# A T5 attention and snake-MLP kernel on one core: regrouped first loads, band rows from a DRAM table, float32 values cast on POOL, two tokens a row, full-row warm-up

## Chip, cores and metric

The kernel runs on one core of one Trainium2 chip. The metric is the device time of one execution in microseconds (us). Engines: PE is TensorE, PEld its weight loads, DVE VectorE, ACT ScalarE, POOL GpSimd, SP the engine that here only issues loads and stores (SPq, ACTq, POOLq: the queue side of an engine). "Granted clock" is the share of TensorE's full clock that the throttle allowed.

## The reference

```python
# attention: q, k, v are [8 batches, 8 heads, 576 tokens, 64], float32
scores = (q @ k.T) / sqrt(64) + bias_table[bucket(|i - j|)]     # 32 buckets
attn   = softmax(scores);  o = attn @ v                         # per batch and head
# MLP over the 4608 tokens x 512: w_in [512, 2048], w_out [2048, 512]
h   = x @ w_in
g   = h + sin(alpha * h) ** 2 / alpha
out = g @ w_out                                                 # float32
```

## The kernel before

It takes the batches one after the other, each as four pairs of heads. It multiplies the exponentials of the raw scores by exponentials of the bias (DVE), which depend only on i - j: `m2` holds for each head 128 rows of 384 values, row p being a table of 512 values shifted by p ("band rows"); `mh` holds two pieces of it rearranged. Batches 0 and 1 have their k and q transposed on PE from natural-order tiles (`nat0`: the first pair, `nat1`: the other pairs of batch 0, `nat2`: batch 1). The order on each engine is set ahead by a planner in the program, which uses estimated durations and a few start times (`T_...`). The parts that the change and the argument touch:

```python
SI = 4; SN = (128, 16); SO = (0, 512)     # 4 tokens to a partition row: 512 + 64 tokens

# --- SP queue: bias table, then k and q of the first pair ---
nc.sync.dma_start(out=tabN, in_=bias_table)
nc.sync.dma_start(out=tabL, in_=...)                        # its last row, 32 times
for kq, src in ((0, k), (1, q)):
    load_nat([x[:, kq] for x in nat0], src[0], 0, 2, eng=nc.sync)
# --- POOL queue (casts float32 to float16 on the way) ---
... nat1, pair 1 ...
load_v16(0)                                                 # values of batch 0
... nat1, heads 4 to 7 ...

def warm(n):                                                # warm-up matmuls, 64 rows
    x = new_mo()
    for _ in range(n):
        nc.tensor.matmul(out=x, lhsT=kzs[0][0:64, 0, S : S + 128],
                         rhs=kzs[0][0:64, 0, S : S + 512], start=True, stop=True)

nc.scalar.activation(out=tabE, in_=tabN, func=AF.Exp)
warm(WARM0)
nc.tensor.matmul(out=eps_[0:H, 0:EW], lhsT=tabE, rhs=phi_sb, start=True, stop=True)
warm(WARM1)
nc.scalar.activation(out=e_sb, in_=eps_[0:H, 0:EW], func=AF.Copy)   # 8 x 512 table, SBUF
for h in range(H):                                          # 8 loads, SBUF to SBUF
    nc.sync.dma_start(out=m2[:, h, :],
        in_=bass.AP(tensor=e_sb.tensor, offset=e_sb[h : h + 1, 127:128].offset,
                    ap=[[e_sb.ap[0][0], 1], [-1, 128], [1, XW]]))
nc.sync.dma_start(out=alphaN, in_=...)
nc.sync.dma_start(out=idf_sb, in_=idf.ap())
# --- POOL, in order ---
nc.gpsimd.tensor_copy(out=mh[0:64, :, :], in_=me[0:64, 0, :, 0:192])
nc.gpsimd.tensor_copy(out=mh[64:128, :, :], in_=me[64:128, 1, :, 64:256])
load_w_in16()
... nat2 (batch 1), values of batch 1, w_out ...

# --- copies of a transposed k or q tile out of PSUM: one for each row size (128, 16) ---
for j in range(2):
    n, o = SN[j], SO[j]
    pin = c.v[:, o : o + SI * n].rearrange("d (i p) -> d i p", i=SI)
    ...
        copy_on(e, cols(kzs[t], o)[0:64], pin[0:64])
# ... cut: scores, exponentials, averages, MLP, planner
```

The softmax here doesn't subtract the row's maximum and nothing guards it: scores larger than these inputs give would overflow.

## Time and profile before

| quantity (before) | value |
|---|---|
| device time, median of 3 | 489.86 us (488.75 to 490.55) |
| PE busy over the span | 94% |
| PE busy in the first 40 us | 19.3 us |
| a steady batch, 142.26 to 192.89 us | 50.63 us, PE busy 50.48 |
| `mh` copies done | 36.7 us |
| first MoE matmul (`sc<-xT,w_in`) | 68.70 us |

First, three lines of the page's slices. The span is cut in 40 slices of 12.2 us; a digit is the busy share in tenths, for PEclk the granted clock.

```profile
PE   5268979999999999999999999999999999999996
...
PEclk9997979999999999999999999999999999999999
DMA  9969999940990099309960699039001000000021
```

From the seventh slice to the last but one PE is at nine tenths, so a microsecond won in front is won at the end, as long as the later part doesn't change. PE had little to do early (5, 2, 6) while the DMA engines looked busy.

The windows view gives PE's busy time, the granted clock, the DMA share and the rate in stretches: the first 40 us, the MoE-in stage of batch 0, and a steady batch.

```profile
core 0: us, PE busy (x) PEld busy (x) DVE busy (x) ACT busy (x) POOL busy (x), PEclk, DMA share, GB/s
0.00:40.00 40.00, 19.34 (x151) 9.59 (x151) 14.86 (x30) 15.34 (x32) 14.04 (x24) 0.95 1.09 81
67.50:89.90 22.40, 21.16 (x138) 9.67 (x139) 19.31 (x34) 18.79 (x32) 7.64 (x7) 0.87 1.99 164
142.26:192.89 50.63, 50.48 (x346) 25.61 (x345) 30.06 (x64) 44.36 (x98) 9.24 (x8) 1.00 0.80 90
```

The chain of waits, cut at 45 us and in order of time (start, length, what): line 405 is the loop of eight band-row loads, line 410 a small load issued behind them.

```profile
4.99 0.60 ACT e_sb L403
...
5.60 0.65 SPq L405
...
8.78 5.97 SPq L405
...
27.28 3.77 SPq L410
...
31.10 4.72 DMA idf_sb<-identf
...
35.87 0.84 POOL mh L414
```

Issuing eight loads kept SP from 5.6 to 27.3 us: five of the eight issues lasted 1.8 to 6.0 us. The profile doesn't name what they waited for; earlier loads are likely, since the eight issues of e12 below took 4.4 us in all. The waits view up to 45 us (engine and line, what was waited for, total us, times, longest) shows who stood still for it:

```profile
POOL mh L413 <- DMA m_77<-e_sb: 23.8, 1, 23.8
...
PE mo L470 <- DMA nat_128_95<-in_k_dram: 8.9, 1, 8.9
...
DVE u L564 <- POOL mh L414: 7.4, 1, 7.4
PE mo L470 <- DVE kz_66 L450: 6.2, 1, 6.2
```

Three microseconds in which little but band rows moves (the DMA view from 24 to 27 us; packets, MB, share of 16 engines):

```profile
DMA packets 155, 0.10 MB, mean 34 GB/s; under 512 B 7, under 2 KB 155, under 8 KB 155
...
q1 hardware_dynamic: 110, 0.08, 73.2%
```

The q1 packets are the band rows: 0.732 x 16 engines x 3 us / 110 = 0.32 us for a packet of 768 bytes in this quiet stretch. Over all 1,024 row packets of the trace the mean is 0.24 us.

### The profile page before, as it was taken

The numbers are of one execution on the slowest core, as the hardware profiler recorded it, in microseconds if no ns is written. First come the engines' busy times: TensorE is split into PE (matmuls) and PEld (weight loads), VectorE is DVE, ScalarE is ACT, GpSimd is POOL, SyncE is SP. The second block draws the span as 40 slices with busy tenths as digits, with TensorE's granted clock in tenths as the row PEclk, the third lists the DMA queues.
The fourth block names the chain that finished last, engine by engine and source line by source line (L and its number), as shares of the span: only waits on it lengthen the run. The fifth ranks groups of instructions, "written<-read, shape, count | busy, mean of one in ns | idle before, by whom it ended". The sixth has DMA issues, their size and how long they took to land.

```text
span 488.1 us, 8297 instructions
## 1 busy us (share of the span) xinstructions
PE 456.9 (94%) x3133; PEld 229.1 (47%) x3133; DVE 277.5 (57%) x580; ACT 388.7 (80%) x838; POOL 83.3 (17%) x88
## 2 busy tenths in 40 slices
PE   5268979999999999999999999999999999999996
PEld 2134434455445544554455545554455445544442
DVE  4229568645674468445854494449544864479700
ACT  4255979987898879887997799779987998799711
POOL 7016774000700061004300340012000000000000
PEclk9997979999999999999999999999999999999999
DMA  9969999940990099309960699039001000000021
GB/s 119 96 27 174 152 184 153 178 85 23 176 159 24 22 145 158 54 24 105 170 64 21 108 156 92 24 94 145 23 23 44 1 23 21 33 13 0 23 80 71
DMA packets 140295, 40.09 MB, mean 82 GB/s; under 512 B 124336, under 2 KB 135136, under 8 KB 140256
## 3 DMA queue, kind: packets, MB, share of 16 engines
q0 software_dynamic: 100000, 18.06, 48.1%
q1 hardware_dynamic: 40064, 21.45, 22.5%
q8 instruction: 24, 0.39, 0.3%
q14 instruction: 15, 0.12, 0.1%
q10 hardware_dynamic: 192, 0.07, 0.1%
HBM read 36.78 MB, written 16.52 MB: 109 GB/s over the span
## 4 chain that ended last, share of the span: by engine, by line
PE 62%; ACT 24%; issue 6%; SPq 5%; DVE 1%; DMA 1%; POOL 0%; ACTq 0%; DVEq 0%
PE mo L717 20%; PE av L613 15%; PE sc L541 13%; PE sc L669 8%; PE av L607 5%; SPq L405 4%; ACT u L548 4%; ACT L738 3%; ACT sq L683 2%; DMA idf_sb<-identf 1%; PE mo L470 1%; ACT kz_67 L448 1%; SPq L410 1%; DVE kz_67 L450 1%; ACT rd L633 1%
## 5 line engine op out<-in xcount | busy, mean ns | idle before, releaser
L548 ACT ACTIVATE u<-sc 128x384 f16<-128x384 f32 x448 | 173.0, 544 | 17.9 <-PE sc L541 17.7
L717 PE MATMUL mo<-w_out_80,g 128*128 128x512 f16 x576 | 173.7, 379 | 0.0
L669 PE MATMUL sc<-xT,w_in_79 128*128 128x512 f16 x576 | 132.8, 384 | 0.9 <-DVE g L690 0.9
L581 DVE TENSOR_TENSOR u<-u,m_77 128x512 f16<-128x512 f16 (+1 forms) x192 | 71.3, 390 | 72.4 <-ACT u L548 71.2
L690 DVE SCALAR_TENSOR_TENSOR g<-sq,inv_a,sc 128x512 f16<-128x512 f16 x144 | 104.5, 747 | 3.9 <-ACT sq L683 1.1
L669 PEld LDWEIGHTS <-w_in_79 128*128 128x128 f16 x576 | 56.1, 99 | 69.3 <-issue 4.4
L717 PEld LDWEIGHTS <-g 128*128 128x128 f16 x576 | 55.7, 97 | 53.4 <-issue 4.3
L541 PE MATMUL sc<-qT_69,kz_66 128*128 128x384 f16 (+1 forms) x288 | 63.2, 298 | 1.0 <-ACT u L548 0.2
L541 PE MATMUL sc<-qT_70,kz_67 128*128 128x384 f16 (+1 forms) x288 | 63.7, 285 | 0.2
L629 ACT ACTIVATE lnd<-av 128x384 f32<-128x384 f32 x64 | 27.2, 425 | 42.0 <-PE av L613 42.0
L644 DVE TENSOR_TENSOR xT<-av,rd 128x384 f16<-128x384 f32 (+1 forms) x68 | 29.4, 437 | 48.6 <-ACT rd L633 32.6
L613 PE MATMUL av<-u,ones 128*64 128x192 f16 (+1 forms) x512 | 43.8, 293 | 0.0
L334 POOL DMA_DIRECT2D v_72<-in_v_dram x16 | 14.1, 889 | 131.1 <-PE av L613 124.8
L541 PEld LDWEIGHTS <-kz_66 128*128 128x128 f16 x288 | 26.5, 100 | 20.9 <-issue 5.0
L541 PEld LDWEIGHTS <-kz_67 128*128 128x128 f16 x288 | 26.7, 97 | 19.8 <-issue 0.8
L334 POOL DMA_DIRECT2D v_71<-in_v_dram x16 | 15.3, 1106 | 82.9 <-PE av L613 82.8
L450 DVE COPY outs<-mo 128x512 f32<-128x512 f32 x28 | 19.2, 687 | 17.7 <-PE mo L717 17.6
L633 ACT ACTIVATE rd<-lnd 128x384 f32<-128x384 f32 x64 | 28.2, 440 | 1.3
L613 PEld LDWEIGHTS <-ones 128*64 128x64 f16 x512 | 21.7, 109 | 13.4 <-issue 7.4
L613 PE MATMUL av<-u,v_71 128*64 128x384 f16 (+1 forms) x256 | 21.8, 292 | 0.0
L613 PE MATMUL av<-u,v_72 128*64 128x384 f16 (+1 forms) x256 | 21.8, 292 | 0.0
L448 ACT ACTIVATE outs<-mo 128x512 f32<-128x512 f32 x8 | 4.8, 597 | 20.6 <-PE mo L717 20.6
(359 smaller groups left out, 403.8 us busy)
## 6 DMA issues: line engine op xcount, KB each, us to landing
out_dram<-outs SPq DMA_DIRECT2D x36, 256.0 KB, 2.0
staged_k<-in_k_dram POOLq DMA_DIRECT2D x6, 576.0 KB, 13.6
staged_q<-in_q_dram POOLq DMA_DIRECT2D x6, 576.0 KB, 15.8
v_71<-in_v_dram POOLq DMA_DIRECT2D x16, 128.0 KB, 8.1
w_in_79<-in_moe_w_in_dram POOLq DMA_DIRECT2D x4, 512.0 KB, 8.1
v_72<-in_v_dram POOLq DMA_DIRECT2D x16, 128.0 KB, 5.4
w_out_80<-in_moe_w_out_dram POOLq DMA_DIRECT2D x4, 512.0 KB, 9.6
kz_66<-kraw SPq DMA_DIRECT2D x3, 288.0 KB, 6.0
```

The source lines that it names most:

```text
L334: nc.gpsimd.dma_start(out=vs[t % 2][:, c], in_=vp[128 * c : 128 * c + 128],)
L541: nc.tensor.matmul(out=sc.v[:, n * y : n * y + n], lhsT=kzs[t % 2][:, p, k0 : k0 + 128], rhs=qTs[t % 2][:, p, q0 : q0 + n], start=True, st ...
L548: nc.scalar.activation(out=u.v[:, k0 : k0 + nc_, q0 : q0 + n], in_=sc.v[:, 0 : n * nc_], func=AF.Exp, scale=0.125,)
L581: nc.vector.tensor_tensor(out=io, in0=io, in1=m2[:, 2 * p : 2 * p + 2, x0 : x0 + hi - lo], op=ALU.mult,)
L607: nc.tensor.matmul(out=o[:, 0:n], lhsT=vhs[t % 2][:, p] if y else ones2, rhs=u.v[:, 8, q0 : q0 + n], start=True, stop=False,)
L613: nc.tensor.matmul(out=o[64 * z : 64 * z + 64, 0:n], lhsT=vs[t % 2][:, c, 2 * p + z, :] if y else ones, rhs=u.v[:, 4 * z + c, q0 : q0 + n] ...
L629: nc.scalar.activation(out=ln.v[:, 0:n], in_=avs[0].v[:, 0:n], func=AF.Ln)
L633: nc.scalar.activation(out=rd.v[:, 0:n], in_=ln.v[:, 0:n], func=AF.Exp, scale=-1.0)
L644: nc.vector.tensor_tensor(out=xT[:, p, (x0 + a) % XN : (x0 + a) % XN + m - a], in0=avs[1].v[:, a:m], in1=rd.v[:, a:m], op=ALU.mult,)
L669: nc.tensor.matmul(out=h.v, lhsT=w_in16[:, j, 128 * f : 128 * f + 128], rhs=xT[:, j, 512 * b % XN : 512 * b % XN + 512], start=(j == 0), s ...
L690: nc.vector.scalar_tensor_tensor(out=gcell[b].v[:, f, :], in0=sq.v, scalar=inv_a[:, f : f + 1], in1=h.v, op0=ALU.mult, op1=ALU.add,)
L717: nc.tensor.matmul(out=m.v, lhsT=gcell[b].v[:, f, 128 * a : 128 * a + 128], rhs=w_out16[:, f, :], start=(f == 0), stop=(f == NF - 1),)
```

## The change

Its intent is to start PE's real work earlier. The small bias table is written to DRAM and the band rows are read from there in one load, in ascending order; POOL then copies them reversed. The first k load goes ahead of the table on SP, q on ACT's queue, `nat1` alone on POOL's queue; the values come as float32 over SP and POOL casts them. k and q rows hold two tokens instead of four, which makes the copies out of PSUM single. Warm-up matmuls use 128 rows. The planner's start times are moved. The diff is cut to its core; several lines are pressed into one in places, and `<...>` or `...` stands for what is left out.

```diff
-T_START = 9.0   T_M2 = 14.0  T_V0 = 15.0  T_TR1 = 38.0  T_W = 33.0  T_WO = 56.0
+T_START = 8.0   T_M2 = 13.0  T_V0 = 17.0  T_TR1 = 36.0  T_W = 28.0  T_WO = 50.0
-    SI = 4;  SN = (128, 16);  SO = (0, 512)
+    SI = 2;  SN = (128, 128, 32);  SO = (0, 256, 512)
+    e_dram = nc.dram_tensor("e_dram", [H, EW], F16, kind="Internal")
+    # vst, vhst (float32 values) and m2r (rows): room in w_out16, which is loaded later
+    def cast_v(eng, t):
+        for c in range(4):
+            eng.tensor_copy(out=vs[t][:, c], in_=vst[:, c])
+        ...
+    def warm(n):                    # zz: 128 x 512 zeros
+            nc.tensor.matmul(out=x, lhsT=zz[:, 0:128], rhs=zz, start=True, stop=True)
+    load_nat(nat0, 0, 0, 2, k[0], nc.sync)          # ahead of tabN, tabL
     nc.sync.dma_start(out=tabN, in_=bias_table)
     nc.sync.dma_start(out=tabL, ...)
+    load_nat(nat0, 1, 0, 2, q[0], nc.scalar)
     ... nat1 on POOL ...
-    load_v16(0)
-    nc.scalar.activation(out=e_sb, in_=eps_[0:H, 0:EW], func=AF.Copy)
-    for h in range(H):
-        nc.sync.dma_start(out=m2[:, h, :], in_=<e_sb, partition h, rows descending>)
+    nc.vector.tensor_copy(out=e_sb, in_=eps_[0:H, 0:EW])
+    nc.sync.dma_start(out=e_dram.ap(), in_=e_sb)
+    nc.sync.dma_start(
+        out=m2r, in_=bass.AP(tensor=e_dram, offset=0, ap=[[1, 128], [EW, H], [1, XW]]))
+    load_v32(0, nc.sync)
+    for p in range(NP):
+        nc.gpsimd.tensor_copy(
+            out=m2[:, 2 * p : 2 * p + 2, :], in_=m2r[:, 2 * p : 2 * p + 2, ::-1])
     nc.gpsimd.tensor_copy(out=mh[0:64, ...)  ; nc.gpsimd.tensor_copy(out=mh[64:128, ...)
+    cast_v(nc.gpsimd, 0)
     load_w_in16()
     ... nat2 ...
     # copies out of PSUM: one over all 576 tokens
-        for j in range(2): ... copy_on(e, cols(kzs[t], o)[0:64], pin[0:64]) ...
+        put(kzs[t][:, p, 0:S], slice(0, 64), 0, 288)
     # ... cut: casts of the first pair, memsets moved to POOL, values of batch 1
```

More of the change, by code (lines that the diff above doesn't have):

```diff
@@ L160 @@
 OFFSET = 8
-T_START = 9.0
-T_M2 = 14.0
-T_V0 = 15.0
-T_TR1 = 38.0
-T_W = 33.0
-T_WO = 56.0
+T_START = 8.0
+T_M2 = 13.0
+T_V0 = 17.0
+T_TR1 = 36.0
+T_W = 28.0
+T_WO = 50.0
 WARM0 = 5
@@ L210 @@
     WIN = ((0, 384), (384, 192))
-    SI = 4
-    SN = (128, 16)
-    SO = (0, 512)
+    SI = 2
+    SN = (128, 128, 32)
+    SO = (0, 256, 512)
     XN = 1536
@@ L246 @@
     w_out16 = sgl.tile([128, NF, DM], F16, name="w_out16")
+    wv = w_out16.rearrange("p f n -> p (f n)")
+    vst = wv[:, 0 : 2 * 4 * H * D].bitcast(F32).rearrange("p (c h d) -> p c h d", c=4, h=H)
+    vhst = wv[:, 2 * 4 * H * D : 2 * 4 * H * D + 2 * NP * D].bitcast(F32).rearrange(
+        "p (hp d) -> p hp d", hp=NP
+    )
+    m2r = wv[:, 2 * 5 * H * D : 2 * 5 * H * D + H * XW].rearrange("p (h x) -> p h x", h=H)
+    zz = sgl.tile([128, 512], F16, name="zz")
     alphaT = sgl.tile([128, NF], F32, name="alphaT")
@@ L264 @@
     natx = tp.tile([128, NF * DM], F16, name="natx", tag="g", bufs=2)
-    N0 = 2 * 2 * SI * D
-    nat0 = [
-        natx[0:n, 2 * N0 * i : 2 * N0 * (i + 1)].bitcast(F32).rearrange(
-            "s (kq h x) -> s kq h x", kq=2, h=2
-        )
-        for i, n in enumerate(SN)
-    ]
-    natb = [
-        natx[0:n, 4 * N0 + N0 * i : 4 * N0 + N0 * (i + 1)].rearrange(
-            "s (kq i two d) -> s kq i two d", kq=2, i=SI, two=2
-        )
-        for i, n in enumerate(SN)
-    ]
-    nat2x = tp.tile([128, NF * DM], F16, name="nat2", tag="g", bufs=2)
-    N2 = 2 * H * SI * D
-    nat2 = [
-        nat2x[0:n, N2 * i : N2 * (i + 1)].rearrange("s (kq h x) -> s kq h x", kq=2, h=H)
-        for i, n in enumerate(SN)
-    ]
-    nat1 = [sgl.tile([n, 2, H - 2, SI * D], F16, name=f"nat1_{n}") for n in SN]
+    N0 = 3 * 2 * 2 * SI * D
+    nat0 = natx[:, 0 : 2 * N0].bitcast(F32).rearrange(
+        "s (j kq h x) -> s j kq h x", j=3, kq=2, h=2
+    )
+    natb = natx[:, 2 * N0 : 3 * N0].rearrange(
+        "s (j kq i two d) -> s j kq i two d", j=3, kq=2, i=SI, two=2
+    )
+    nat2x = tp.tile([128, NF * DM], F16, name="nat2", tag="g", bufs=2)
+    nat2 = nat2x[:, 0 : 3 * 2 * H * SI * D].rearrange(
+        "s (j kq h x) -> s j kq h x", j=3, kq=2, h=H
+    )
+    nat1 = sgl.tile([128, 3, 2, H - 2, SI * D], F16, name="nat1")
     def new_g():
@@ L341, in load_v16, with load_v32, load_nat @@
             )
-    def load_nat(dst, src, h0, h1, parts=(0, 1), eng=None):
-        for i in parts:
-            n, o = SN[i], SO[i]
-            (eng or nc.gpsimd).dma_start(
-                out=dst[i],
+    def load_v32(t, eng):
+        vp = v[t].rearrange("h s d -> s h d")
+        for c in range(4):
+            eng.dma_start(out=vst[:, c], in_=vp[128 * c : 128 * c + 128])
+        vq = v[t].rearrange("(hp two) s d -> two s hp d", two=2)
+        for z in range(2):
+            eng.dma_start(out=vhst[64 * z : 64 * z + 64], in_=vq[z, 512:S])
+    def cast_v(eng, t):
+        for c in range(4):
+            eng.tensor_copy(out=vs[t][:, c], in_=vst[:, c])
+        for z in range(2):
+            eng.tensor_copy(
+                out=vhs[t][64 * z : 64 * z + 64, :, z, :], in_=vhst[64 * z : 64 * z + 64]
+            )
+    def load_nat(dst, kq, h0, h1, src, eng, parts=(0, 1, 2)):
+        for j in parts:
+            n, o = SN[j], SO[j]
+            eng.dma_start(
+                out=dst[0:n, j, kq],
                 in_=src[h0:h1, o : o + SI * n].rearrange("h (p i) d -> p h (i d)", i=SI),
@@ L361, in load_w_out16, with clear_v, cast0 @@
             )
-    nc.scalar.dma_start(out=phi_sb, in_=phi_h.ap())
-    nc.scalar.dma_start(out=id_sb, in_=idm.ap())
-    nc.scalar.preload_act_table_set(EXP_SET)
+    def clear_v(eng, i):
+        eng.memset(vhs[i][0:64, :, 1, :], 0.0)
+        eng.memset(vhs[i][64:128, :, 0, :], 0.0)
+    def warm(n):
+        x = new_mo()
+        for _ in range(n):
+            nc.tensor.matmul(out=x, lhsT=zz[:, 0:128], rhs=zz, start=True, stop=True)
+    def cast0(kq, j, eng):
+        n = SN[2 * j]
+        for jj in (0, 1) if j == 0 else (2,):
+            o = natb[0:n, jj, kq]
+            i_ = nat0[0:n, jj, kq].rearrange("s two (i d) -> s i two d", i=SI)
+            if eng is nc.scalar:
+                eng.activation(out=o, in_=i_, func=AF.Copy)
+            else:
+                eng.tensor_copy(out=o, in_=i_)
+    load_nat(nat0, 0, 0, 2, k[0], nc.sync)
     nc.sync.dma_start(out=tabN, in_=bias_table)
@@ L371 @@
     )
+    nc.scalar.dma_start(out=phi_sb, in_=phi_h.ap())
+    load_nat(nat0, 1, 0, 2, q[0], nc.scalar)
+    nc.scalar.dma_start(out=id_sb, in_=idm.ap())
+    nc.scalar.preload_act_table_set(EXP_SET)
     for kq, src in ((0, k), (1, q)):
-        load_nat([x[:, kq] for x in nat0], src[0], 0, 2, eng=nc.sync)
+        load_nat(nat1[:, :, :, 0:2], kq, 2, 4, src[0], nc.gpsimd, parts=(0, 1))
     for kq, src in ((0, k), (1, q)):
-        load_nat([x[:, kq, 0:2] for x in nat1], src[0], 2, 4, parts=(0,))
+        load_nat(nat1, kq, 2, H, src[0], nc.gpsimd, parts=(2,))
     for kq, src in ((0, k), (1, q)):
-        load_nat([x[:, kq] for x in nat1], src[0], 2, H, parts=(1,))
-    load_v16(0)
-    for kq, src in ((0, k), (1, q)):
-        load_nat([x[:, kq, 2:6] for x in nat1], src[0], 4, H, parts=(0,))
+        load_nat(nat1[:, :, :, 2:6], kq, 4, H, src[0], nc.gpsimd, parts=(0, 1))
+    nc.vector.memset(zz, 0.0)
     nc.vector.memset(kzs[0][0:64, :, S : 2 * S], 0.0)
-    def warm(n):
-        x = new_mo()
-        for _ in range(n):
-            nc.tensor.matmul(
-                out=x, lhsT=kzs[0][0:64, 0, S : S + 128], rhs=kzs[0][0:64, 0, S : S + 512],
-                start=True, stop=True,
-            )
-    def clear_v(eng, i):
-        eng.memset(vhs[i][0:64, :, 1, :], 0.0)
-        eng.memset(vhs[i][64:128, :, 0, :], 0.0)
-    nc.vector.memset(kzs[0][64:128, :, 0:S], 0.0)
     nc.vector.tensor_tensor(out=tabN, in0=tabN, in1=tabL, op=ALU.subtract)
@@ L402 @@
     warm(WARM1)
-    nc.scalar.activation(out=e_sb, in_=eps_[0:H, 0:EW], func=AF.Copy)
-    for h in range(H):
-        nc.sync.dma_start(
-            out=m2[:, h, :],
-            in_=bass.AP(tensor=e_sb.tensor, offset=e_sb[h : h + 1, 127:128].offset,
-                        ap=[[e_sb.ap[0][0], 1], [-1, 128], [1, XW]]),
-        )
+    nc.vector.tensor_copy(out=e_sb, in_=eps_[0:H, 0:EW])
+    nc.sync.dma_start(out=e_dram.ap(), in_=e_sb)
+    cast0(0, 0, nc.vector)
+    cast0(1, 0, nc.scalar)
+    cast0(0, 1, nc.vector)
+    cast0(1, 1, nc.scalar)
+    nc.vector.memset(kzs[0][64:128, :, 0:S], 0.0)
+    nc.sync.dma_start(
+        out=m2r, in_=bass.AP(tensor=e_dram, offset=0, ap=[[1, 128], [EW, H], [1, XW]])
+    )
+    load_v32(0, nc.sync)
     nc.sync.dma_start(out=alphaN, in_=moe_alpha.rearrange("(f p) -> f p", p=128))
     nc.sync.dma_start(out=idf_sb, in_=idf.ap())
+    clear_v(nc.gpsimd, 0)
+    nc.gpsimd.memset(ones, 1.0)
+    nc.gpsimd.memset(ones2, 0.0)
+    nc.gpsimd.memset(ones2[0:64, 0, :], 1.0)
+    nc.gpsimd.memset(ones2[64:128, 1, :], 1.0)
+    for p in range(NP):
+        nc.gpsimd.tensor_copy(
+            out=m2[:, 2 * p : 2 * p + 2, :], in_=m2r[:, 2 * p : 2 * p + 2, ::-1]
+        )
     me = m2.rearrange("p (hp two) x -> p two hp x", two=2)
@@ L414 @@
     nc.gpsimd.tensor_copy(out=mh[64:128, :, :], in_=me[64:128, 1, :, 64:256])
+    cast_v(nc.gpsimd, 0)
     load_w_in16()
     for kq, src in ((0, k), (1, q)):
-        load_nat([x[:, kq] for x in nat2], src[1], 0, H)
+        load_nat(nat2, kq, 0, H, src[1], nc.gpsimd)
+    load_v32(1, nc.sync)
     clear_v(nc.gpsimd, 1)
-    load_v16(1)
     nc.gpsimd.memset(kzs[1][0:64, :, S : 2 * S], 0.0)
     nc.gpsimd.memset(kzs[1][64:128, :, 0:S], 0.0)
+    cast_v(nc.gpsimd, 1)
     load_w_out16()
-    def cast0(kq):
-        for i in range(2):
-            i_ = nat0[i][:, kq].rearrange("s two (i d) -> s i two d", i=SI)
-            if kq == 0:
-                nc.vector.tensor_copy(out=natb[i][:, kq], in_=i_)
-            else:
-                nc.scalar.activation(out=natb[i][:, kq], in_=i_, func=AF.Copy)
-    cast0(0)
-    cast0(1)
-    clear_v(nc.vector, 0)
-    nc.vector.memset(ones, 1.0)
-    nc.vector.memset(ones2, 0.0)
-    nc.vector.memset(ones2[0:64, 0, :], 1.0)
-    nc.vector.memset(ones2[64:128, 1, :], 1.0)
     plan = Plan()
@@ L457, in mm @@
             c.v = new_mo().bitcast(F16)
-            for j in range(2):
-                n, o = SN[j], SO[j]
+            for j in range(3):
+                n = SN[j]
                 for i in range(SI):
-                    x = o + n * i
+                    x = i * (S // 2) + SO[j] // 2
                     if t == 0 and p == 0:
                         nc.tensor.transpose(
-                            out=c.v[:, x : x + n], in_=natb[j][:, kq, i],
+                            out=c.v[:, x : x + n], in_=natb[0:n, j, kq, i],
                             identity=id_sb[0:n, 0:n],
@@ L471, in mm @@
                             out=c.v[64 * z : 64 * z + 64, x : x + n],
-                            in_=(nat1 if t == 0 else nat2)[j][:, kq, h, D * i : D * i + D],
+                            in_=(nat1 if t == 0 else nat2)[0:n, j, kq, h, D * i : D * i + D],
                             identity=id_sb[0:n, 0:n],
@@ L477, in go, with put @@
             def go(e):
-                for j in range(2):
-                    n, o = SN[j], SO[j]
-                    pin = c.v[:, o : o + SI * n].rearrange("d (i p) -> d i p", i=SI)
-                    def cols(tile, c0):
-                        return tile[:, p, c0 : c0 + SI * n].rearrange("d (p i) -> d i p", i=SI)
-                    if kq == 1:
-                        copy_on(e, cols(qTs[t], o), pin)
-                    elif part == 0:
-                        copy_on(e, cols(kzs[t], o)[0:64], pin[0:64])
-                    else:
-                        copy_on(e, cols(kzs[t], (S + 64, S)[j])[64:128], pin[64:128])
+                pin = c.v[:, 0:S].rearrange("d (i p) -> d i p", i=SI)
+                def put(dst, r, p0, p1):
+                    copy_on(
+                        e, dst.rearrange("d (p i) -> d i p", i=SI)[r], pin[r][:, :, p0:p1]
+                    )
+                if kq == 1:
+                    put(qTs[t][:, p, :], slice(0, 128), 0, 288)
+                elif part == 0:
+                    put(kzs[t][:, p, 0:S], slice(0, 64), 0, 288)
+                else:
+                    put(kzs[t][:, p, S + 64 : 2 * S], slice(64, 128), 0, 256)
+                    put(kzs[t][:, p, S : S + 64], slice(64, 128), 256, 288)
             return go
         m = plan.add({"PE": 0.4 if t == 0 and p == 0 else 0.7}, mm, deps, pri, nb, new=[b])
-        eng = {"DVE": 0.95, "ACT": 0.85}
+        eng = {"DVE": 0.75, "ACT": 0.7}
         return [plan.add(eng, cp(x), [m], pri, use=[b]) for x in range(1 if kq else 2)]
```

## The prediction

> **What bounds it now.** By the page's slices TensorE (PE) is saturated from about 40 us to the end (94% of the span; a steady batch takes 50.6 us). The change leaves that part alone. The loss is in front: the windows view gives PE 19.3 us of work in the first 40 us, 5 of it warm-up.
>
> 47% of the chain of waits in the first 45 us is the SP queue issuing eight band-row loads (`m2` from `e_sb`, 5.6 to 27.3 us; each 8.6–15.7 us to landing). POOL stands 23.8 us before the `mh` copies (34.7 us); the band multiply with `mh` waits 7.4 us for them, and pair 2's transposes 6.2 us for in-order DVE: PE resumes at 38.5 us. Earlier PE waits 8.9 us (to 24.8) for `nat1` heads 4–7, queued behind the values. `w_in` and later POOL loads start only at 36.65 us. While only band rows remain (24–27 us), a packet costs 0.32 us (73% of 16 engines x 3 us, 110 packets).
>
> **What changes.**
> - Band rows come from DRAM in one load. 1,024-byte DRAM rows took about 52 ns a packet at 3–6 us; 1,024 packets then take 3–4 us, not 20. Price: a DRAM write (2 us), four reversing POOL copies (0.8 us each, sized like the `mh` copies), a table behind the `k` load. Expected: e_sb at 7.5 us, rows landed 14.5, `mh` 20.
> - Values arrive as float32 on SP and are cast on POOL (3 us), ready near 23 us. `nat1` lands by 13: its wait vanishes.
> - Two tokens a row: 12 transposes instead of 16 per tile (0.15 us less), single copies (0.8 instead of 1.4 us), but twice the packets at half the size. [...] `nat` rows are now written as 256 B, values too. Before, 128-byte rows moved at about 1,000 packets/us at 55–58 us, so no disaster.
> - Full-row warm-up: no time of its own.
>
> **The sum.** First scores at 11.4 instead of 13.6 us. First values product at 23 instead of 30.5; PE then skips the 6.2 us stop and has 2 us of transposes behind it: 15–16 us ahead. The rest of batch 0 stays bound by ACT and PE (first MoE matmul 68.8 us before); 1–2 us come off for slow-clock matmuls and copies. Batch 1's `nat2` follows the value cast and `w_in` on POOL and lands at 42–46 us, when PE wants it at 42–43: I charge 2–3 us. Net 16.4 us; the first MoE matmul comes at about 52 us.
>
> All of it is on the critical path, since PE is saturated afterwards: 489.9 - 16.4 = **473.5 us, 80% range 466 to 482**. Faster by over 2%: 0.86; within 2%: 0.135; slower: 0.005.
>
> **Signs.** Right: band rows leave the chain's head; PE idle before 40 us falls by 10 us or more; no PE wait for `nat1`; `mh` at 18–22 us; `w_in` issued at 22–26; first MoE matmul at 49–56; steady batches unchanged. The granted clock fell to 0.50 after the 6 us stop (36–40 us) and at 68–72; the first dip should go [...]. Wrong: `mh` after 26 us, or first MoE matmul after 60.
>
> **What would make it wrong.** 256-byte float32 packets slow on SP, values after 28 us; reversing or casting copies slower on POOL; `nat2` later than that, PE stopped before the last averages; a lasting clock dip. If none bites, 466.

The sum came to 16.4 us. The 2 us of the DRAM write and the 3 us of the casts are estimates; in the trace before, the stores of 256 KB took 2.0 us from issue to landing and an `mh` copy (64x768) 0.82 us.

## The result, and the profile after

The changed kernel took **472.89 us** (median of 4 runs, 471.44 to 473.53), beside 489.73 us of the kernel before (median of 4). The ratio is 0.9653 with a 95% interval of 0.9623 to 0.9683. Ratios here are the mean time of one kernel's fast runs over that of the other's of the same rounds, so they are not quite the ratio of the medians quoted.

The same slices (now of 11.8 us), windows, chain and waits:

```profile
PE   5688899999999999999999999999999999999996
...
PEclk9989899999999999999999999999999999999999
DMA  9699999409900996049901990094101000100021
```

```profile
core 0: us, PE busy (x) PEld busy (x) DVE busy (x) ACT busy (x) POOL busy (x), PEclk, DMA share, GB/s
0.00:40.00 40.00, 28.54 (x235) 13.83 (x237) 19.87 (x43) 25.02 (x63) 29.27 (x46) 0.96 0.98 176
54.89:73.16 18.27, 17.82 (x119) 8.25 (x120) 15.77 (x29) 17.26 (x28) 8.73 (x8) 1.00 2.06 163
125.73:176.36 50.63, 50.48 (x346) 25.57 (x345) 30.06 (x64) 44.37 (x98) 9.24 (x8) 1.00 0.82 92
44.00:48.00 4.00, 2.27 (x27) 1.27 (x26) 2.32 (x7) 3.70 (x10) 4.00 (x5) 1.00 1.31 164
48.00:52.00 4.00, 3.95 (x26) 1.54 (x26) 0.00 (x0) 1.83 (x3) 2.98 (x2) 0.57 1.12 168
```

PE does 28.5 us of work in the first 40 us instead of 19.3. A steady batch takes 50.63 us as before, to the hundredth. The MoE-in stage of batch 0 got shorter too, and it ran at full clock (1.00 instead of 0.87). At 44 to 48 us PE stands again for a while (1.2 us at the longest), and its clock falls to 0.57 behind it.

```profile
3.24 3.45 DMA tabL<-in_bias_table_dram
...
8.48 3.08 DMA e_dram<-e_sb
...
11.58 4.22 DMA w_out_80<-e_dram
...
15.93 3.71 POOL m_77 L446 x4
...
19.71 0.90 POOL mh L450
...
21.56 2.44 POOL v_71 L354 x4
...
25.40 9.01 DMA w_in_79<-in_moe_w_in_dram
...
34.69 13.60 DMA nat_95<-in_q_dram
```

The chain is now a relay: the last row of the bias table lands at 6.7 us behind the k load, the table (8 KB) goes to DRAM in 3.1 us and comes back as rows in 4.2 us (the trace calls the room `w_out_80`), POOL reverses (0.93 us on average for 128x768 float16), copies `mh`, casts the values (0.61 us on average for 128x512), and only then issues `w_in` and `nat2`. The last `nat2` load (named `nat_95`) lands at 48.3 us.

```profile
PE av L631 <- POOL vh_73 L356: 3.8, 1, 3.8
...
POOL nat_95 L364 <- DMA w_in_79<-in_moe_w_in_dram: 3.6, 2, 1.8
```

In the waits view up to 60 us, the wait for `nat1` (8.9 us) and the stop at 38 us (6.2 us) are gone. In their place PE waits 3.8 us for the value casts, up to 24.98 us. The band rows, seen from 12 to 15 us in the DMA view:

```profile
q1 hardware_dynamic: 944, 0.72, 81.4%
```

That is 0.814 x 16 x 3 us / 944 = 41 ns a packet, an eighth of the 0.32 us before.

A ledger helps with the experiments. ACT loads the Sin table when the attention of batch 0 ends, and the Exp table again when batch 0's MoE-in stage ends; these two instructions cut every span in three. The ledger takes one profiled execution of each kernel. The runs of one kernel differ by up to 2.4 us, so a difference of 1 to 2 us between two rows tells little by itself:

| run | attention of batch 0 until | MoE-in stage | rest | span |
|---|---|---|---|---|
| before | 66.22 | 23.68 | 398.2 | 488.1 |
| after | 53.61 | 19.55 | 398.4 | 471.6 |
| e1_rows_only | 52.82 | 23.90 | 398.1 | 474.8 |
| e2_rows_back | 73.57 | 19.55 | 398.6 | 491.7 |
| e12_eight_loads_dram | 52.26 | 23.07 | 398.2 | 473.5 |
| e13_ascending_sbuf | 67.76 | 23.81 | 398.2 | 489.8 |
| e3_values_by_dma | 50.82 | 19.55 | 398.1 | 468.5 |
| e4_four_tokens | 53.01 | 22.71 | 398.4 | 474.1 |
| e5_warm64 | 52.24 | 19.55 | 398.4 | 470.2 |
| e6_old_times | 50.61 | 20.62 | 398.5 | 469.7 |
| e7_nat2_first | 48.33 | 19.56 | 398.4 | 466.3 |
| e9_table_first | 50.88 | 19.55 | 398.5 | 468.9 |
| e10_both | 50.57 | 19.55 | 398.5 | 468.6 |
| e11_three | 47.88 | 19.55 | 398.2 | 465.6 |

The rest is the same in all of them (398.1 to 398.6). The change won 12.6 us in the attention of batch 0 and 4.1 us in the stage behind it.

### The profile page after: what moved, and what is told of

It is laid out like the page before. It is cut to its first block, busy times and chain, and to the rows that moved or that the text cites. A ratio compares the mean times of both kernels' runs of the same rounds, so it can differ in the third digit from the quotient of the medians.

```text
span 471.6 us, 8180 instructions
## 1 busy us (share of the span) xinstructions
PE 452.2 (96%) x3073; PEld 225.6 (48%) x3073; DVE 269.2 (57%) x565; ACT 383.4 (81%) x834; POOL 91.1 (19%) x104
## 4 chain that ended last, share of the span: by engine, by line
PE 60%; ACT 23%; DMA 8%; issue 5%; POOL 2%; DVE 2%; ACTq 0%; POOLq 0%; DVEq 0%
PE mo L741 21%; PE av L637 15%; PE sc L565 12%; PE sc L693 6%; PE av L631 5%; ACT L762 4%; DMA nat_95<-in_q_dram 3%; ACT sq L707 3%; ACT u L572 2%; DMA w_in_79<-in_moe_w_in_dram 2%; DMA w_out_80<-e_dram 1%; POOL m_77 L446 1%; DVE g L714 1%; DMA tabL<-in_bias_table_dram 1%; DMA e_dram<-e_sb 1%
## 5 line engine op out<-in xcount | busy, mean ns | idle before, releaser
L693 PE MATMUL sc<-xT,w_in_79 128*128 128x512 f16 x576 | 130.5, 379 | 0.3 <-DVE g L714 0.3
L605 DVE TENSOR_TENSOR u<-u,m_77 128x512 f16<-128x512 f16 (+1 forms) x192 | 73.8, 402 | 73.6 <-ACT u L572 72.0
L693 PEld LDWEIGHTS <-w_in_79 128*128 128x128 f16 x576 | 55.5, 98 | 66.9 <-issue 0.6
L565 PEld LDWEIGHTS <-kz_66 128*128 128x128 f16 x288 | 25.9, 98 | 22.1 <-issue 6.1
L565 PEld LDWEIGHTS <-kz_67 128*128 128x128 f16 x288 | 26.7, 97 | 19.8 <-issue 0.8
L335 POOL DMA_DIRECT2D v_72<-in_v_dram x12 | 10.6, 894 | 122.2 <-PE av L637 122.2
L473 DVE COPY outs<-mo 128x512 f32<-128x512 f32 x28 | 19.3, 688 | 18.3 <-PE mo L741 18.3
L335 POOL DMA_DIRECT2D v_71<-in_v_dram x12 | 10.6, 894 | 86.2 <-PE av L637 86.2
L637 PE MATMUL av<-u,v_71 128*64 128x384 f16 (+1 forms) x256 | 23.1, 304 | 0.0
L637 PE MATMUL av<-u,v_72 128*64 128x384 f16 (+1 forms) x256 | 21.8, 292 | 0.0
L471 ACT ACTIVATE outs<-mo 128x512 f32<-128x512 f32 x8 | 4.8, 597 | 20.6 <-PE mo L741 20.6
```

What stands on the lines that cost most here:

```text
L335: nc.gpsimd.dma_start(out=vs[t % 2][:, c], in_=vp[128 * c : 128 * c + 128],)
L565: nc.tensor.matmul(out=sc.v[:, n * y : n * y + n], lhsT=kzs[t % 2][:, p, k0 : k0 + 128], rhs=qTs[t % 2][:, p, q0 : q0 + n], start=True, st ...
L605: nc.vector.tensor_tensor(out=io, in0=io, in1=m2[:, 2 * p : 2 * p + 2, x0 : x0 + hi - lo], op=ALU.mult,)
L637: nc.tensor.matmul(out=o[64 * z : 64 * z + 64, 0:n], lhsT=vs[t % 2][:, c, 2 * p + z, :] if y else ones, rhs=u.v[:, 4 * z + c, q0 : q0 + n] ...
L693: nc.tensor.matmul(out=h.v, lhsT=w_in16[:, j, 128 * f : 128 * f + 128], rhs=xT[:, j, 512 * b % XN : 512 * b % XN + 512], start=(j == 0), s ...
```

## The experiments

The main theory, M, was that the gain comes from where the band rows are read: small reads from single on-chip partitions are slow (0.32 us a packet in the window above), and SP, POOL and, behind them, everything else of the first 40 us waited for them. The rivals: R1, the gain comes from the regrouped queues and the float32 values (no wait for `nat1`); R2, a large part comes from two tokens a row; R3, it is the planner's new start times; R4, it is one load instead of eight; R5, it is ascending instead of descending reads. All kernels gave correct results.

### The band rows alone, and everything but them

Kernel before with the rows through DRAM and the reversing copies, nothing else:

```diff
+    nc.sync.dma_start(out=e_dram.ap(), in_=e_sb)
-    for h in range(H): nc.sync.dma_start(out=m2[:, h, :], in_=<e_sb, descending>)
+    nc.sync.dma_start(out=m2r, in_=<e_dram, all heads, ascending>)
+    <4 reversing POOL copies m2r -> m2>
```

> The kernel before, with one part of the change: the band rows go to DRAM, come back in one load and are reversed by four POOL copies. Theory M (the eight loads out of single rows of on-chip memory clog the engines of the DMA and hold SP and POOL; nearly all of the gain is theirs): rows landed at about 15.5 us, mh done at 20 to 22, w_in issued at 21 to 23, nat1 heads 4-7 landed by about 17 since the values no longer share the engines with slow packets, so PE does not stop for it; 470 to 476 us. Rival R1 (the gain is in the regrouping: values off the POOL queue): PE still waits for nat1 until about 24 us and the time is 479 to 485. Rival R2 (the gain is in two tokens a row, with its single copies): 482 to 487.

It took 476.03 us, ratio 0.9716 (0.9693 to 0.9740), at the upper edge of M's range (470 to 476). The attention of batch 0 ended 13.4 us earlier, as much as in the whole change (12.6) within what repeats differ by, and the stage behind it stayed at 23.9. So this part alone is enough for the attention's gain, and it explains none of the stage's. R1 falls as the main cause: the regrouped queues aren't in this kernel. The rows landed later than expected (17.8 instead of 15.5 us), because the table's write took 4.4 us and the rows 7.7 us beside the loads of POOL's queue.

The changed kernel with the rows from on chip again, and the values issued ahead of them on SP:

```diff
-    nc.sync.dma_start(out=e_dram.ap(), in_=e_sb)
-    nc.sync.dma_start(out=m2r, in_=<e_dram>)
     load_v32(0, nc.sync)
+    for h in range(H): nc.sync.dma_start(out=m2[:, h, :], in_=<e_sb, descending>)
-    <4 reversing POOL copies>
```

> The changed kernel with that one part undone: the eight loads from e_sb straight into m2, no reversing copies; the float32 values are issued on SP ahead of them so that they do not queue behind. Theory M: issues of the rows stretch from about 8.5 to about 28 us, mh done at 32 to 36, w_in issued after 35; 482 to 488 us. R1: more than half of the gain stays, 475 to 480. R2: 472 to 477.

It took 493.69 us, ratio 1.0085 (1.0057 to 1.0113). This missed the range: it is slower than the kernel before. The SP and POOL lines of its timeline (start, length, what, idle before and releaser) say why:

```profile
13.10 21.11 SPq L434 DMA_DIRECT2D m<-e_sb  x8
```

```profile
41.68 0.82 POOL L447 COPY mh<-m 64x768 f16<-64x768 f16 x1 [31.28 <-DMA alphaN<-in_moe_alpha_dram]
```

The six value loads held SP until 13.0 us, and the eight row loads then took as long to issue as before (21.1 us), so `mh` was ready at 44.5 us and the cast values at 47.9 us. The short stage (19.55 us) is there all the same. The direction agrees with M; the amount shows that in-order queues add such delays up.

### Source, number of loads or direction

Kernel before, rows from DRAM but in eight loads (one look, state unknown):

```diff
+    nc.sync.dma_start(out=e_dram.ap(), in_=e_sb)
     for h in range(H):
-        nc.sync.dma_start(out=m2[:, h, :], in_=<e_sb, partition h, descending>)
+        nc.sync.dma_start(out=m2r[:, h, :],
+            in_=bass.AP(tensor=e_dram, offset=EW * h, ap=[[1, 128], [1, XW]]))
+    <4 reversing POOL copies>
```

> The kernel before with the rows from DRAM, but in eight loads, one a head, instead of one. Theory M (what is slow is reading out of single rows of on-chip memory, not the count of loads): packets at 40 to 60 ns, SP done with the issues within 5 us, mh done by 25 us; 474 to 479 us. Rival R4 (eight separate loads and their issue are what is slow): issues stretch over 15 us or more, mh after 30; 484 or more.

475.31 us. Its timeline on SP and its DMA view from 12 to 15 us:

```profile
10.42 4.41 SPq L409 DMA_DIRECT2D w_out<-e_dram  x8
```

```profile
q1 hardware_dynamic: 183, 0.13, 18.4%
```

Eight issues take 4.4 us, and a packet 0.184 x 48 us / 183 = 48 ns, although other traffic fills the engines. R4 falls.

Kernel before, eight loads from on chip but ascending, with the reversing copies (one look, state unknown):

```diff
     for h in range(H):
-        nc.sync.dma_start(out=m2[:, h, :],  in_=<e_sb, offset 127, step -1>)
+        nc.sync.dma_start(out=m2r[:, h, :], in_=<e_sb, offset 0, step 1>)
+    <4 reversing POOL copies>
```

> The kernel before with the eight loads from e_sb, but read in ascending steps and reversed afterwards by the four POOL copies. Theory M (the source row in on-chip memory is the slow thing): packets at 0.25 to 0.35 us as before, mh done 3 us later than before, at 38 to 40 us; 489 to 494 us. Rival R5 (the descending step is what is slow): packets below 0.15 us, mh by 30 us; 476 to 484.

491.56 us, no gain at all. Its timeline on SP and its DMA view from 27 to 30 us:

```profile
5.60 21.77 SPq L407 DMA_DIRECT2D w_out<-e_sb  x8
```

```profile
q1 hardware_dynamic: 111, 0.08, 77.9%
```

0.779 x 48 / 111 = 0.34 us a packet. R5 falls. With the number of loads and the direction the same, these two kernels differ in the source, and in the write to DRAM that goes with it; the packets differ by a factor of seven in these windows. Over all 1,024 row packets of each trace the means are 41 ns and 0.23 us.

Why these reads from on chip are so slow was not tried further. In the kernel before, 8 x 96 KB = 786,432 bytes were read between the first issue at 5.6 us and about 34.7 us, each load from one partition: 27.0 GB/s, an estimate from these two times. Reading the table from copies in several partitions would test whether the single partition sets that rate; no run did. But the trace of the kernel before holds other loads from on chip to on chip: later batches copy `kraw` into `kz` on the same SP queue, from 64 partitions at once. Its DMA view from 233 to 235 us, where these are nearly all of q1:

```profile
q1 hardware_dynamic: 471, 0.49, 99.4%
```

That is 0.994 x 16 x 2 us / 471 = 68 ns a packet of about 1 KB. So a source on chip isn't slow as such (68 ns here, 0.32 us for the band rows); that a single partition is what makes it slow fits this, but no run changes that alone. A load from DRAM whose partition step descends would save the reversing copies; no run has one.

### The other parts of the change, one by one

The changed kernel with the values loaded and cast by POOL's queue, as before, but behind `nat1`:

```diff
-    load_v32(0, nc.sync)
+    load_v16(0)                       # on POOL's queue, behind nat1
-    cast_v(nc.gpsimd, 0)
     ... batch 1 likewise ...
```

> The changed kernel with the values loaded and cast by the POOL queue's DMA as before, but behind nat1; no POOL casts. Theory M: with no slow row packets the values land at 17 to 19 us, the cast of 3.4 us on POOL is saved, w_in is issued at about 22.5 instead of 24.9, the first values product comes at about 22 instead of 25; 468 to 472 us, so that this part of the change cost time. R1: the POOL queue is the trouble, values land after 24 us and the time is 476 or more.

470.10 us, ratio 0.9597 (0.9571 to 0.9623): in the range, but not by the path expected. The POOL lines of its timeline:

```profile
19.23 3.71 POOL L446 COPY m<-w_out 128x768 f16<-128x768 f16 x4 [4.44 <-DMA w_out<-e_dram]
...
23.93 0.84 POOL L451 COPY mh<-m 64x768 f16<-64x768 f16 x1
```

The rows land 3.3 us later than in the changed kernel, beside the values on POOL's queue, and the first values product comes at 25.8 us instead of the expected 22. `w_in` is issued at 24.73 us, as late as with the casts, so POOL's time isn't what was won. But the last `nat2` load lands at 44.8 instead of 48.3 us, and PE's stop for `nat2` is gone. The changed kernel's DMA view from 24 to 27 us shows a likely reason (q0 is POOL's queue, with `w_in` since 24.87 us; q1 moves batch 1's values):

```profile
q1 hardware_dynamic: 3163, 0.80, 117.6%
q0 software_dynamic: 1, 0.00, 1.7%
```

Batch 1's float32 values, issued on SP from 22.3 us, went ahead of `w_in`, and `nat2` came behind both; in e3 the DMA engines were idle from 20 to 24 us, just ahead of it. No run moved these values alone, so this cause isn't shown. The float32 part of the change, then, gained nothing; e3's interval lies clear of the one of e5 below (0.9630 to 0.9672), which behaves as the changed kernel does, but the two were in different rounds.

The changed kernel with four tokens a row and the old two-part copies:

```diff
-    SI = 2;  SN = (128, 128, 32);  SO = (0, 256, 512)
+    SI = 4;  SN = (128, 16);       SO = (0, 512)
     <tiles, transposes and copies as in the kernel before>
```

> The changed kernel with four tokens a row again (16 transposes a tile, two copies instead of one, rows of 1,024 bytes). Theory M: every copy is 0.6 us longer, first scores 1 to 1.5 us later, and the copies of batch 1 cost 1 to 2 us; the loads are no faster where it matters; 475 to 478 us. R2: at least half of the gain goes, 481 us or more. If half-size packets cost more than the copies save: 468 to 472.

476.05 us, ratio 0.9723 (0.9699 to 0.9747), in the expected range, but not by all of the expected steps: the first scores came only 0.6 us later (13.68 us). The attention ends where it did (53.0 us), and the stage is 3.2 us longer. These are PE's timeline lines just ahead of the stage, before, after and in this run:

```profile
67.82 0.95 PE L470 MATMUL mo<-id_sb,nat_94 128*64 128x128 f16 x16 [2.59 <-DVE kz_67 L450]
68.70 7.71 PE L669 MATMUL sc<-xT,w_in_79 128*128 128x512 f16 x24
```

```profile
55.03 0.58 PE L493 MATMUL mo<-id_sb,nat_95 128*64 128x128 f16 x12 [0.67 <-DVE kz_67 L473]
55.54 5.35 PE L693 MATMUL sc<-xT,w_in_79 128*128 128x512 f16 x24
```

```profile
54.61 0.95 PE L498 MATMUL mo<-id_sb,nat 128*64 128x128 f16 x16 [2.31 <-DVE kz L478]
55.49 6.72 PE L697 MATMUL sc<-xT,w_in 128*128 128x512 f16 x24
```

With four tokens, PE stands 2.3 to 2.6 us for a DVE copy that comes in two instructions (1.29 and 0.33 us); then the clock is low (0.50 from 68 to 72 us before, 0.66 on average from 50 to 60 us in e4) and 24 matmuls take 6.7 to 7.7 us. With the single copy (0.8 us) the stop is 0.7 us, the clock stays at 1.00 and the same 24 take 5.35 us. From the first of them to the end of the stage, the kernel before takes 3.6 us and e4 2.6 us longer than the changed kernel, and these 24 account for 2.4 and 1.4 us of that; the rest wasn't taken apart. R2 is therefore right about the stage behind the attention (3.2 of its 4.1 us in this pair of profiles; in the ledger every kernel with four tokens has 22.7 to 23.9 us there, every one with two 19.5 to 20.6) and wrong about the rest.

The first MoE matmul comes at the same time in both (55.49 and 55.54 us). In the waits view from 36 to 56 us PE waits for `nat2` in the changed kernel (1.5 us in two places) and never in e4: with four tokens POOL issues `nat2` in four loads, all by 29.1 us, and with two tokens in six, the last at 34.69 us after two stops behind `w_in`. So two tokens a row traded the stop for the copies against a late `nat2`, and their gain is what comes behind.

Warm-up matmuls over 64 rows again, and the planner's old start times, each in the changed kernel:

```diff
-    nc.tensor.matmul(out=x, lhsT=zz[:, 0:128],     rhs=zz, ...)
+    nc.tensor.matmul(out=x, lhsT=zz[0:64, 0:128],  rhs=zz[0:64, :], ...)
```

> The changed kernel with warm-up matmuls over 64 rows of zeros instead of 128, nothing else. Theory M: no time of its own; within 1 us of the changed kernel (472 to 474 us). [...]

472.59 us, ratio 0.9651 (0.9630 to 0.9672): no effect on the time, as expected. The rival cut from the text rested on a mechanism of the clock that no trace shows; it expected longer first scores and a time up by 1 us or more. The first four scores did take 1.46 us here and 0.82 us in the changed kernel, but 1.46 us also in e3, with full rows.

```diff
-T_START = 8.0   T_M2 = 13.0  T_V0 = 17.0  T_TR1 = 36.0  T_W = 28.0  T_WO = 50.0
+T_START = 9.0   T_M2 = 14.0  T_V0 = 15.0  T_TR1 = 38.0  T_W = 33.0  T_WO = 56.0
```

> The changed kernel with the six planner times (start, band, values, transposes and weights of batch 1) of the kernel before, so that only the order on the engines can change. Theory M: the order hardly matters while the loads decide; 472 to 475 us. Rival R3 (the re-planned order is a real part of the gain): 476 or more.

471.16 us, ratio 0.9622 (0.9601 to 0.9642), slightly below the expected range, and its interval overlaps that of e5 in the same rounds. R3 falls: the new times give none of the gain. With the old ones, the transposes from `nat2` stand behind more averages and PE has no stop for them (attention until 50.61 us), but the stage is 1.1 us longer.

### What the changed kernel still loses

`nat2` issued ahead of `w_in` on POOL's queue:

```diff
-    load_w_in16()
     for kq, src in ((0, k), (1, q)):
         load_nat(nat2, kq, 0, H, src[1], nc.gpsimd)
+    load_w_in16()
```

> The changed kernel with batch 1's nat2 issued on POOL ahead of w_in instead of behind it. Theory M (the late nat2 is a new wait: it landed at 45 to 48 us, PE stopped in front of and between the transposes, and the clock dipped at 48 to 52 us): nat2 lands before 40 us, the dip goes, the Sin table is loaded at 50.5 to 52 us instead of 53.6; 469.5 to 471.5 us. If the wait was hidden under ScalarE: 472 to 474. If w_in then comes too late: 475 or more.

469.41 us, ratio 0.9582 (0.9557 to 0.9607), just below the expected range and 3.2 us below e5 in the same rounds with intervals apart. Its four runs lie in two pairs (468.1 and 468.5, 470.3 and 470.5), and the profile is of the fastest. The windows that answer to those of the changed kernel at 44 to 52 us:

```profile
44.00:48.00 4.00, 3.60 (x55) 2.06 (x51) 1.70 (x4) 3.40 (x9) 4.00 (x3) 1.00 1.19 200
48.00:52.00 4.00, 3.33 (x41) 1.84 (x40) 2.78 (x6) 3.81 (x5) 3.44 (x5) 1.00 1.23 203
```

The loads landed 6 to 8 us after their issue, by 36 us, and neither the stop nor the fall of the clock is there. So the order behind POOL's queue cost the changed kernel about 3 us. An estimate from its trace splits that in halves: its own stop for `nat2` is 1.5 us in all, and the four groups of averages from 48.5 us on took 3.88 us at the low clock (0.57 from 48 to 52 us), where the same groups took 2.34 us from 38.67 us.

The bias table ahead of the first k load on SP:

```diff
+    nc.sync.dma_start(out=tabN, in_=bias_table)
+    nc.sync.dma_start(out=tabL, ...)
     load_nat(nat0, 0, 0, 2, k[0], nc.sync)
-    nc.sync.dma_start(out=tabN, in_=bias_table)
-    nc.sync.dma_start(out=tabL, ...)
```

> The changed kernel with the two small loads of the bias table issued on SP ahead of the first k instead of behind it, as before the change. Theory M (the chain table, e_sb, DRAM write, rows, reversal, mh, value cast decides until 25 us): e_sb at about 6 instead of 8.5 us, rows landed at 13.3, values ready at 22.5, all later loads 2.5 us earlier; 469.5 to 471.5 us. If the values' landing (20 us) or nat1 decides: 472 to 474.

470.99 us, ratio 0.9621 (0.9600 to 0.9643). The time is in the range, the steps only half: `e_sb` was ready 2.3 us earlier (6.1 us), but the row load (issued at 8.62 us) now ran beside the `nat1` loads and took 6.6 us, so the rows came only 0.6 us earlier (15.2 us) and the values at 24.1 us. Its interval overlaps that of e5.

Both together, and both with the values cast by DMA as in e3 (issued behind POOL's memsets):

> The changed kernel with nat2 ahead of w_in and the table loads ahead of the first k together. Theory M: nat2 first took out 3 us; the table first brought e_sb forward by 2.4 us but the rows only by about 0.6, since they then shared the engines with nat1; so the two together gain little over nat2 first alone: 467.5 to 469.5 us. If the two gains add up in full: 466 to 467.5.

> As the run with both, and in addition the values loaded and cast by POOL's queue behind nat1 and the small memsets, without float32 copies and POOL casts. Theory M (POOL's work between the rows and w_in is on the chain; the cast is 3.4 us of it): nat2 issued at about 21 us, Sin table at 46 to 48 us; 465 to 467.5 us. If the values then share the engines with the rows and push mh back as far as the cast cost, as in the run with values by DMA (mh 3.3 us later): 467.5 to 470.

The first took 470.65 us, ratio 0.9609 (0.9593 to 0.9625): a miss. All its four runs lie within 0.7 us, and its profile shows a long fall of the clock:

```profile
16.00:20.00 4.00, 3.48 (x35) 2.48 (x32) 3.77 (x6) 1.99 (x6) 3.94 (x5) 0.50 0.78 174
...
24.00:28.00 4.00, 3.59 (x18) 1.41 (x20) 0.86 (x2) 1.20 (x3) 4.00 (x6) 0.50 1.28 238
```

The granted clock stayed at 0.50 from 16 to 28 us, with PE busy 3.48, 2.00 and 3.59 us of each four; from 14.7 to 22.0 us PE had a single stop, of 0.52 us. In the changed kernel the clock was 1.00 from 12 to 24 us. What brings about such a difference isn't shown. By the clock records of the two kernels and the windows of e9 and e10, the stretches at 0.50 last 3.4 us (the changed kernel), 6.8 (the kernel before), 10.2 (e9) and 17.1 us (e10), all close to multiples of 3.41 us. In the kernel before one began at 35.9 us, in PE's 6.2 us stop; in e7 one (14.6 to 21.4 us) began when PE had not stopped for longer than 0.9 us since 9.7 us. But the fall isn't shown to be what e10 lost by: over its four runs the mean granted clock goes from 0.982 to 0.991, and the run at 0.991 (470.53 us) was no faster than the profiled one at 0.982 (470.33 us). Why e10 gained nothing over e7 stays open.

The second took **466.65 us**, ratio 0.9524 (0.9505 to 0.9543), as expected; it beats both kernels, and its interval lies clear of all others here. Its attention ends at 47.88 us.

## Why the prediction was right, and where its terms were off

The time was predicted as 473.5 us and came as 472.89. The mechanism held: the band rows left the head of the chain, and e1, e12 and e13 show that reading them from DRAM, not the number of loads or their order, is what did it. But the total came out by errors that offset each other, and the sum as written doesn't add up: 15 to 16 us ahead, plus 1 to 2, less 2 to 3, gives 13 to 16 us and not 16.4.

| term | predicted | measured in the changed kernel |
|---|---|---|
| `e_sb` | 7.5 us | 8.45 us |
| rows landed | 14.5 us | 15.8 us |
| `mh` | 20 us | 21.5 us |
| values ready | 23 us | 24.9 us |
| first scores | 11.4 us | 13.04 us |
| `nat1` | lands by 13 us, no wait | no wait |
| first values product (30.5 before) | 23 us | 24.98 us |
| ahead behind it | 15 to 16 us | 13.1 us |
| cost of late `nat2` | 2 to 3 us | about 3.2 us (e7 against e5) |
| first MoE matmul (68.7 before) | 52 us | 55.54 us |
| gained after that | nothing ("all later work" shifts) | 3.6 us |
| whole | 16.4 us | 16.5 us between the two profiled spans |

**The first step that was off** is "e_sb at 7.5 us". Its cause is the order on SP's queue: the last row of the table waited behind the k load and landed at 6.7 us. Everything of the relay came 1 to 2 us late, the values at 24.9 instead of 23 us. Of these 1.9 us, 0.95 are `e_sb`; the write and the row load add 0.35, POOL's copies 0.2 and the casts 0.4. Here "ahead" is read at the last ten exponentials of the last pair: they start at 56.14 us before and at 43.07 us after. The missing 2 us stand at the values, as e9 partly confirms: with the table first they came 0.8 us earlier.

**The second** is what the prediction counted for single copies and a slow clock: "1–2 us come off" ahead of the first MoE matmul, and everything after that "shifts". Between those exponentials and the first MoE matmul nothing came off on balance: 12.56 us before, 12.47 after. e4 shows both sides of that: no wait for `nat2`, the stop for the copy instead, and the same first MoE matmul. The saving came behind it. From the first MoE matmul to the end of the stage, 21.20 us became 17.62: the two-part copies had stopped PE 2.6 us just ahead of that stage, the clock had been 0.50 from 68 to 72 us, and the prediction had named that second fall without counting it as avoidable. e4 shows both come back with four tokens (a stop of 2.3 us, a mean clock of 0.66 from 50 to 60 us).

The 3.6 us that were not foreseen made good for the 3.5 us by which the first MoE matmul came later than predicted. A prediction whose total is right within 1 us was here built on terms that were wrong by 2 to 4 us and on a sum that they don't give. The mechanism was understood; that the total fits so closely is luck.

**The signs.** `mh` at 18 to 22 us, `w_in` issued at 22 to 26 us (24.87), the first MoE matmul at 49 to 56 us, unchanged steady batches and no wait for `nat1` came as predicted. PE's idle time before 40 us fell by 9.2 us (from 20.66 to 11.46), not by 10 or more. The clock's fall at 36 to 40 us went, but another at 24 to 28 us (0.59) took its place behind PE's 3.8 us wait for the values, and a third at 48 to 52 us (0.57).

**The values in float32.** The prediction took them as part of the way to 23 us. They did not help: e3 without them was 2.8 us faster by the medians of different rounds. That batch 1's values would go ahead of `w_in` was not foreseen.

**Packet sizes.** 256-byte packets were feared for the values and for the `nat` rows. No PE wait for `nat1` came of them, and the values' own load wasn't what the casts waited for: POOL went from the `mh` copies to the casts without a stop. `nat2` did come late, as predicted, with more loads to issue behind `w_in` and with `w_in` behind batch 1's values; the share of its packets' size in that was not measured.

## What to carry to other kernels

When a load is late although few bytes move, divide the engines' busy time by the packets: 0.32 us beside 41 ns told here that reading this source was slow, where the busy share alone looked like full bandwidth. When the head of a saturated kernel gets shorter, also read the next stage that the same copies feed, for it may hold a stop and a low clock of its own (2.6 us and 0.50 here); and don't take a correct total as proof of the terms. Behind a serial queue, order the loads by who needs them first: the same loads in another order were worth 3 us here.
